# A Strassen-style scheme for four of six chunks of a decay attention with a two-layer softplus network

## The chip, the cores and the metric

The kernel runs on one core of a Trainium2 chip. The metric is the device time in microseconds (us) of one execution; the times given are medians over runs. The profile is of one execution, taken by the hardware profiler.

## What is computed

Causal attention with a per-head decay, for 4 batches, 8 heads, 768 positions and head size 64, block by block with a carried state, and then a two-layer network on all 3072 tokens:

```python
# per head: out = (q k^T * Dmask) v + (q * lam_pow) state ; state = lam^64 * state + (k * rev_pow)^T v
x = attn_out.transpose(0, 2, 1, 3).reshape(3072, 512)
h = x @ w_in                                            # 512 -> 2048
g = np.maximum(h, 0.0) + np.log1p(np.exp(-np.abs(h)))   # softplus
return g @ w_out                                        # 2048 -> 512
```

Everything is float32. The two layers do 2 x 3072 x 512 x 2048 multiply-adds.

## The kernel before, in words

The 768 positions are cut into six chunks of 128, so that a chunk has 512 tokens (4 batches x 128). In a chunk, attention is done in four units, one per pair of heads, numbered g = 4 x chunk + pair. Each unit has q, k and v in one SBUF tile of 8 KB per partition.

TensorE multiplies in float32r. To keep float32 accuracy, each operand is split in a high part (a copy rounded by ScalarE) and a low part (VectorE subtracts the high part from the original), and each block product is made from three matmuls: high x high, low x high, high x low. Weights are cut and split once, on the chip, in the first 115 us (`w_scale` to `w_lo`), and then stay in SBUF in sixteen tiles `w_pairs`, two blocks of 128 x 512 each.

The network runs in steps s = 0 to 95, sixteen per chunk. Step s does `mlp1(s)`, 12 matmuls of 512 columns that make 128 rows of the hidden layer in one PSUM bank, and, LAG = 4 steps later, `mlp2([s])`, 12 matmuls that add into four PSUM banks, one per batch. Between the two, `chain_act` (softplus), `chain_hi` (ScalarE) and `chain_lo` (VectorE) turn the bank into the next operand. `finish` does the last batch of the last two steps in two halves of 256 columns, so that each half can be stored on its own.

Up to step 16 the order of all instructions is a list written out by hand. From step 17 on, a loop sets it: at three places of each chunk it puts the next chunk's attention between the steps, `chunk_scores` at f = 3 and `chunk_outs` at f = 7. On each engine, and on SP's DMA queue, instructions run in the order in which the program emits them. Buffers come from pools: "b8" (22 tiles of 8 KB), "b4" (7 of 4 KB), and in PSUM "o" (4 banks), "h" (2 banks), "t" (one tile of 2 banks). GpSimd does ten small instructions at the start and nothing after.

## Time and profile before

| | |
|---|---|
| Time, median of 3 runs (lowest, highest) | 592.29 us (592.20, 592.38) |
| Profiled execution, first to last instruction (span) | 590.3 us |
| TensorE busy (4473 matmuls) | 585.0 us, 99% of the span |
| TensorE weight loads, which overlap the matmuls | 485.7 us, 82% |
| VectorE busy | 252.4 us, 43% |
| ScalarE busy | 233.5 us, 40% |
| GpSimd busy | 1.7 us |
| Moved by DMA | 48.89 MB, mean 83 GB/s |

The span is 1.99 us shorter than the median of the runs: what lies before the first and after the last instruction isn't in it. Matmuls are pipelined, so the mean length of one (390 ns) is longer than the distance from one to the next; the distance is read from the chain or from a window.

### The profile page before, as it was taken

Reading aid. Unit: us, or ns where it says so; the run is one execution under the profiler, and the core shown is the slowest. Engines: PE = TensorE matmul, PEld = TensorE weight load, DVE = VectorE, ACT = ScalarE, POOL = GpSimd, SP = SyncE. Lnnn points to the kernel's source line nnn. Section 1 sums busy time; section 2 is a strip of 40 time slices with the busy share of each in tenths; the row PEclk is TensorE's granted clock in tenths of the full one; section 3 lists DMA queues with packets and bytes.
Section 4 is the critical chain, followed back from the end, with each engine's and each line's share of the span. In section 5 each row is a group of like instructions: output and inputs, shape, how many; then the busy total and the mean of one; then the engine's idle time right before and its main releaser. Section 6 shows DMA issues by size and latency. Waiting matters only on the chain.

```text
span 590.3 us, 10279 instructions
## 1 busy us (share of the span) xinstructions
PE 585.0 (99%) x4473; PEld 485.7 (82%) x4473; DVE 252.4 (43%) x407; ACT 233.5 (40%) x391; POOL 1.7 (0%) x10
## 2 busy tenths in 40 slices
PE   8999999999999999999999999999999999999997
PEld 6878888888888888888888888888888888888886
DVE  7999999658411119621106841012842111201011
ACT  4999966562231363222246132225222122312212
POOL 1000000000000000000000000000000000000000
PEclk9999999999999999999999999999999999999999
DMA  8999502520300211030031030031100000100001
GB/s 298 407 406 410 192 1 73 214 74 1 144 0 1 92 52 73 2 143 1 0 144 72 1 144 1 1 116 44 57 1 2 0 1 0 72 0 1 0 1 71
DMA packets 13294, 48.89 MB, mean 83 GB/s; under 512 B 1474, under 2 KB 1730, under 8 KB 11074
## 3 DMA queue, kind: packets, MB, share of 16 engines
q1 hardware_dynamic: 12816, 47.58, 21.4%
q8 instruction: 35, 0.57, 0.4%
q10 hardware_dynamic: 434, 0.66, 0.3%
q14 instruction: 9, 0.07, 0.0%
HBM read 41.94 MB, written 6.29 MB: 82 GB/s over the span
## 4 chain that ended last, share of the span: by engine, by line
PE 93%; DMA 4%; ACT 2%; DVE 0%; issue 0%
PE o L522 44%; PE h L483 42%; PE z L353 3%; DMA att<-in_att 2%; PE x L322 2%; DMA raw<-in_wts 2%; PE w L322 1%; PE y L326 1%; ACT c L236 0%; ACT raw L240 0%; PE z L364 0%; ACT w L257 0%; PE e L495 0%; PE x L341 0%; PE z L368 0%; DVE w L261 0%
## 5 line engine op out<-in xcount | busy, mean ns | idle before, releaser
L483 PE MATMUL h<-x,w 128*128 128x512 f32 x1152 | 275.4, 390 | 0.2 <-DVE w L261 0.2
L522 PE MATMUL o<-w,g 128*128 128x512 f32 x1146 | 274.4, 390 | 0.0
L483 PEld LDWEIGHTS h<-x,w 128*128 128x128 f32 x1152 | 215.6, 188 | 45.7 <-DVE w L261 0.6
L522 PEld LDWEIGHTS o<-w,g 128*128 128x128 f32 x1146 | 214.6, 188 | 44.9
L472 DVE TENSOR_TENSOR g<-l,g 128x512 fp32r<-128x512 f32 x96 | 66.3, 691 | 308.2 <-ACT g L468 307.9
L464 ACT ACTIVATE l<-h 128x512 f32<-128x512 f32 x96 | 57.4, 598 | 297.2 <-PE h L483 272.2
L468 ACT CAST g<-l 128x512 fp32r<-128x512 f32 x96 | 59.5, 620 | 2.8
L299 ACT ACTIVATE att<-att,rp 64x256 f32<-64x256 f32 x60 | 27.0, 499 | 0.2
L310 DVE TENSOR_TENSOR att<-att,lp 64x512 f32<-64x512 f32 (+1 forms) x42 | 24.6, 585 | 1.1
L375 DVE TENSOR_TENSOR att<-x,mask 64x512 f32<-64x512 f32 (+1 forms) x34 | 19.1, 563 | 5.9 <-PE y L326 4.1
L257 ACT CAST w<-c 128x1024 fp32r<-128x1024 f32 (+1 forms) x19 | 17.2, 912 | 9.3 <-DVE c L254 9.2
L261 DVE TENSOR_TENSOR w<-c,w 128x1024 fp32r<-128x1024 f32 (+1 forms) x19 | 20.0, 1055 | 1.4 <-ACT w L257 1.3
L236 ACT ACTIVATE c<-raw 128x1024 f32<-128x1024 f32 (+1 forms) x19 | 18.9, 997 | 3.9 <-DMA raw<-in_wts 3.7
L254 DVE CUSTOM_DVE_ANT_0 c<-raw,c 128x2048 uint16<-128x2048 uint16 (+1 forms) x19 | 19.8, 1052 | 0.5 <-ACT raw L240 0.4
L248 DVE SCALAR_TENSOR_TENSOR c<-raw,c 128x1024 uint32<-128x1024 uint32 (+1 forms) x19 | 19.9, 1051 | 0.1
L240 ACT ACTIVATE raw<-raw 128x1024 uint32<-128x1024 uint32 (+1 forms) x19 | 18.8, 1005 | 0.0
L353 PE MATMUL z<-att 128*64 128x64 f32 x544 | 17.0, 223 | 0.0
L353 PEld LDWEIGHTS z<-att 128*64 128x64 f32 x544 | 16.3, 138 | 0.6 <-issue 0.4
L396 ACT COPY att<-st 64x512 f32<-64x512 f32 (+1 forms) x21 | 11.0, 535 | 12.2 <-PE y L326 11.3
L322 PEld LDWEIGHTS x<-att 64*64 64x64 f32 x416 | 12.9, 135 | 2.8 <-issue 2.8
L442 ACT CAST x<-z 128x512 fp32r<-128x512 f32 x17 | 9.2, 593 | 13.6 <-PE z L353 9.2
L322 PE MATMUL x<-att 64*64 64x64 f32 x416 | 14.1, 220 | 0.0
(77 smaller groups left out, 223.4 us busy)
## 6 DMA issues: line engine op xcount, KB each, us to landing
att<-in_att SPq DMA_DIRECT2D x17, 1024.0 KB, 6.4
raw<-in_wts SPq DMA_DIRECT2D x32, 512.0 KB, 10.1
out_dram<-ob SPq DMA_DIRECT2D x21, 256.0 KB, 2.5
att<-in_att SPq DMA_DIRECT2D x10, 512.0 KB, 9.6
att<-in_att SPq DMA_DIRECT2D x8, 256.0 KB, 8.7
out_dram<-ob ACTq DMA_DIRECT2D x2, 256.0 KB, 2.0
out_dram<-ob ACTq DMA_DIRECT2D x1, 128.0 KB, 1.8
out_dram<-ob SPq DMA_DIRECT2D x1, 128.0 KB, 1.7
```

The lines of the kernel that those rows point to most:

```text
L248: nc.vector.scalar_tensor_tensor(out=c, in0=raw_at(ks, 1), scalar=0x80000000, in1=c, op0=ALU.bitwise_and, op1=ALU.bitwise_or)
L254: nc.vector.tensor_add(out=c, in0=c, in1=raw_at(ks, 0))
L261: nc.vector.tensor_sub(out=w[:, 1], in0=conv.pop(ks[0]).bitcast(F32), in1=w[:, 0])
L299: nc.scalar.activation(k, k, AF.Copy, scale=rp1[r, h : h + 1])
L310: nc.vector.tensor_mul(out=q, in0=q, in1=w[r, bs])
L322: nc.tensor.matmul(x[to, cols], lhsT=region(g, s)[r, b, t], rhs=region(g, 1 - s)[r, b, t], start=True, stop=True)
L353: nc.tensor.matmul(w[half(t), cols], lhsT=region(g, 2 + s)[:, b, t], rhs=region(g, 1 - s)[:, b, t], start=True, stop=True,)
L464: nc.scalar.activation(l_tiles[s], h_tiles.pop(s), AF.Softplus)
L468: nc.scalar.copy(out=g_tiles[s][:, 0, :], in_=l_tiles[s])
L472: nc.vector.tensor_sub(out=g[:, 1, :], in0=l_tiles.pop(s), in1=g[:, 0, :])
L483: nc.tensor.matmul(h_tiles[s], lhsT=w[:, i, cs], rhs=x[:, j, :], start=p == 0 and n == 0, stop=p == NP - 1 and n == 2,)
L522: nc.tensor.matmul(o_tiles[c][b], lhsT=g[:, i, b * 128 : (b + 1) * 128], rhs=w[:, j], start=f == 0 and n == 0, stop=(f == NF - 1 or s == l ...
```

## The change

Chunks 0 and 1 and the first part of chunk 2's loads stay as they were, up to step 16 of the hand-written list. Chunks 2 and 3, and chunks 4 and 5, are each taken as a pair. In each layer of a pair, the matrices are cut in 2 x 2 blocks, and the product is made from seven block products in place of eight (Strassen's scheme in the form with shared sums).

- **Weights.** `keep` stores three of the seven weight operands of each layer to DRAM as they are. `prepare` makes the other four: GpSimd adds high and low parts of two blocks (2 x 512 columns) and makes four sums or differences (4 x 256 columns), ScalarE and VectorE split the result again, and SP stores it to DRAM. There are 16 such preparations, spread over steps 17 to 34 in program order. All seven operands are then streamed back from DRAM (`l1_load`, `l2_load`), in each pair anew.
- **First layer of a pair**, eight steps j: seven products of 6 matmuls each in three PSUM banks A, B, D. A bank takes a second product after ScalarE (`l1_copy`) or VectorE (`l1_sum`) has read the first. VectorE's sums make the four blocks, ScalarE's softplus runs on them (`soft`). The x operands are seven combinations made by `x_minus` and split by `x_block`.
- **Second layer of a pair**, seven products n in four parts of 12 matmuls: ScalarE and VectorE split the operand (`l2_split`), GpSimd makes the differences of blocks (`l2_minus`, 16 per pair, 1024 columns each), VectorE and ScalarE add up the results (`l2_end`), and SP stores them in four DMAs of 512 KB per pair (`l2_store`). Chunks 2 to 5 are written transposed and turned on the host when the results are collected.
- **Attention** of chunks 2 to 5 is done unit by unit: a burst on TensorE holds the outputs of the last unit and the scores of the next one, five bursts per chunk.
- **Order.** From step 17 on, operations are handed to a planner (`Plan`) with an engine, a booked duration, what they read and write, buffers and a due time. The planner plays them through when the program is built, each engine free to take what is ready, and emits them by the start times that it found. What it emits is fixed from then on.

The diff, cut to its core:

```diff
+    LATENCY = {"PE": 0.35, "ACT": 0.12, "DVE": 0.12, "POOL": 0.15, "SP": 0.1}
...
+                    soonest = min(found)[0]
+                    t, _, n = min((x for x in found if x[0] <= soonest + 0.05), key=lambda x: (x[1], x[2]))
+                    if best is None or t < best[0]:
+                        best = t, n
...
+            if e == "PE":
+                if o["kind"] != last_kind:
+                    dur += 0.14
+                last_kind = o["kind"]
+            free_at[e] = end = t + dur
+            if o["size"] is not None:
+                channel = max(channel, t) + o["size"] / 0.35
+                end = channel + 1.8
...
-    def chunk_scores(c):
...
-    def chunk_outs(c):
...
-    def finish(ss, cols, e, to):
...
+    w1d = dp.tile([NF // 2, 128, 7, 2, 256], F32, name="w1d")
+    w2d = dp.tile([7, 2, 128, 4, 2, 256], F32, name="w2d")
+    def keep(*ks):
+        for k in ks:
+            f, which = w_order[k]
+            w, (j, odd) = w_of(f, which).bitcast(F32), divmod(f, 2)
+            if which == 0:
+                to, of = (w1d[j][:, 2], w[:, :, 256:]) if odd else (w1d[j][:, 0:2].rearrange("q h n e -> q (h n) e").rearrange("q (n h) e -> q n (h e)", n=2), w)
+                nc.sync.dma_start(out=to, in_=of)
+            else:
+                for n, h in ((1, 0), (6, 1)) if odd else ((0, 0),):
+                    nc.sync.dma_start(out=w2d[n, j // 4][:, j % 4], in_=w[:, :, h * 256 : (h + 1) * 256])
...
+        10, shift 24 25, act 11, mlp 12, ghi 11, load 32, keep 1 0 2 3 5 6 7 4 8 9 10 11 12 13 14 15 16 17
+        18 19 20 21, xl1 5, out1 6, hi 22 23, glo 11, act 12, sign 24 25, round 30 31, lo 22 23, keep 22 23,
...
+        sign 28 29, ghi 14, shift 30 31, mlp 16, add 28 29, hi 28 29, unit 10, mlp 15, glo 14, lo 28 29,
+        keep 28 29, mlp2 11, sign 30 31, mlp2 12, mlp2 13, add 30 31, act 15, ghi 15, glo 15, hi 30 31, lo
+        30 31, keep 30 31
...
+    plan = Plan({"b8": 22, "b4": 7, "bl": 1, "bh": 5, "o": 4, "h": 2, "t": 1})
...
+    MM, R6, R12 = 0.2266, 6 * 0.2266, 12 * 0.2266
...
+    def act(n):
+        return 0.15 + 0.0009 * n
+    def dve(n):
+        return 0.16 + 0.00104 * n
+    def pool(n):
+        return 0.25 + 0.0022 * n
+    def ffn(dur, fn, reads, writes, alloc=()):
+        nonlocal clock
+        n = add("PE", dur, fn, reads, (*writes, ("ffn",)), alloc, due=clock)
+        clock += dur
+        return n
...
+    def prepare(which, j):
+        e, o = 2 * j, 2 * j + 1
...
+            nc.gpsimd.tensor_add(
+                out=T8[cs][:, 2 * n : 2 * n + 2].rearrange("q h e -> q (h e)"), in0=w[:, 0], in1=w[:, 1]
+            )
+        for n in range(2):
+            add(
+                "POOL", pool(512), lambda n=n: whole_of(n), [("wp", pairs[n][0])], [(*cs, 2 * n), (*cs, 2 * n + 1)],
+                [("b8", cs), ("b8", sk)] if n == 0 else (), due=due,
+                behind=prepared[-1] if n == 0 and prepared else None,
+            )
+        a11, a12, a21, a22 = (0, 1, 2, 3) if which == 0 else (0, 2, 1, 3)
+        for to, x, y, op in ((6, a21, a22, ALU.add), (7, 6, a11, ALU.subtract), (5, a11, a21, ALU.subtract), (4, a12, 7, ALU.subtract)):
+            def combine(to=to, x=x, y=y, op=op):
+                t = T8[cs]
+                nc.gpsimd.tensor_tensor(out=t[:, to], in0=t[:, x], in1=t[:, y], op=op)
+            add("POOL", pool(256), combine, [(*cs, x), (*cs, y)], [(*cs, to)], due=due)
+        four = [(*cs, n) for n in range(4, 8)]
+        def hi():
+            nc.scalar.copy(out=T8[sk][:, :, 0], in_=T8[cs][:, 4:8])
+        def lo():
+            nc.vector.tensor_sub(out=T8[sk][:, :, 1], in0=T8[cs][:, 4:8], in1=T8[sk][:, :, 0])
+        add("ACT", act(1024), hi, four, [(*sk, 0)], due=due + 6)
+        prepared.append(len(plan.ops))
+        add("DVE", dve(1024), lo, [*four, (*sk, 0)], [(*sk, 1)], due=due + 7)
+        if which == 0:
+            key, to = ("w1d", j), lambda: w1d[j][:, 3:7]
+        else:
+            key, to = ("w2d", j), lambda: w2d[2:6, j // 4, :, j % 4].rearrange("n q a e -> q n a e")
+        add(
+            "SP", 0.06, lambda: nc.sync.dma_start(out=to(), in_=T8[sk].bitcast(F32)), [(*sk, 0), (*sk, 1)], [key], size=1.05,
+            due=due + 8,
+        )
...
+        add("SP", 0.06, load, [], u_keys(g, "q", "k0", "k1", "kt2", "kt3", "v"), [("b8", ("U", g))], size=1.05, due=due, behind=bursts.get(g - 2))
...
+    def attention(c, dues):
+        first = c * NP
+        q = c // 2
+        for g in range(first, first + NP):
+            due = dues[g - first]
+            load_unit(g, due - 5)
+            keys_decay(g, due - 2.5)
+            parts = [scores(g)] if g == first else [outs(g - 1), scores(g)]
+            bursts[g] = burst(parts, due)
+            if g > first:
+                x_copy(g - 1, due + 2)
+            after_scores(g, due + 2)
+        burst([outs(first + NP - 1)], dues[NP])
+        x_copy(first + NP - 1, dues[NP] + 2)
+        end = dues[NP] + 3
+        if c % 2 == 0:
+            x_block(q, 0, c, 0, end)
+            x_block(q, 1, c, 2, end)
+        else:
+            b = c - 1
+            x_minus(q, (b, 0), (c, 0), (b, 0), end)
+            x_block(q, 4, b, 0, end)
+            x_block(q, 2, c, 2, end)
+            x_minus(q, (c, 0), (c, 2), (c, 0), end)
+            x_minus(q, (c, 2), (c, 2), (b, 0), end)
+            x_block(q, 5, c, 2, end)
+            x_block(q, 6, c, 0, end)
+            x_minus(q, (b, 2), (b, 2), (c, 2), end)
+            x_block(q, 3, b, 2, end)
...
+                W1[q, j, n] = t8([128, 4, 2, 256], F32R, f"wa{q}_{j}_{n}")
+                nc.sync.dma_start(out=W1[q, j, n].bitcast(F32)[:, : b - a], in_=w1d[j][:, a:b])
+            add(
+                "SP", 0.06, load, written(0, [j]), [("W1", q, j, n, 0)], [("b8", ("W1", q, j, n))], size=0.262 * (b - a),
+                due=clock - 7, behind=l1_ops.get((q, j - 2) if j > 1 else (q, -1)),
+            )
...
+    def l1_products(q, j, name, wn, xn, to, start):
+        n, i = divmod(wn, 4)
+        def run():
+            if start:
+                AB[q, j, to] = obank(f"{to}{q}_{j}")
+            w, x = W1[q, j, n][:, i], XB[q, xn]
+            if wn < 2:
+                w = W1[q, j, n][:, 0:2].rearrange("q h n e -> q (h n) e").rearrange("q (n h) e -> q n h e", n=2)[:, :, i]
+            for k in range(2):
+                for m, (a, b) in enumerate(((0, 0), (1, 0), (0, 1))):
+                    nc.tensor.matmul(
+                        AB[q, j, to], lhsT=w[:, a, k * 128 : (k + 1) * 128], rhs=x[:, b, k],
+                        start=start and k == 0 and m == 0, stop=k == 1 and m == 2, skip_group_check=not start,
+                    )
...
+    def l1_last(q, j):
+        l1_products(q, j, "P4", 2, 3, "B", False)
+        l1_sum(q, j, "u", "B", blk="21")
+        soft(q, "21", j)
+    l1_ops, l2_ops = {}, []
+    def l1(q, j):
+        l1_ops[q, j] = l1_products(q, j, "P1", 0, 0, "A", True)
+        l1_copy(q, j)
+        if j:
+            l1_last(q, j - 1)
+        l1_products(q, j, "P6", 6, 5, "B", True)
+        l1_sum(q, j, "u", "B", tmp="v")
+        l1_products(q, j, "P5", 5, 4, "D", True)
+        l1_sum(q, j, "u", "D", tmp="d")
+        l1_products(q, j, "P2", 1, 1, "A", False)
+        soft(q, "11", j, "A")
+        l1_products(q, j, "P7", 4, 6, "B", False)
+        l1_sum(q, j, "d", "B", blk="22")
+        soft(q, "22", j)
+        l1_products(q, j, "P3", 3, 2, "D", False)
+        l1_sum(q, j, "v", "D", blk="12")
+        soft(q, "12", j)
+        if j == NF // 2 - 1:
+            l1_last(q, j)
...
+            W2[q, n, h] = t8([128, 4, 2, 256], F32R, f"wb{q}_{n}_{h}")
+            nc.sync.dma_start(out=W2[q, n, h].bitcast(F32), in_=w2d[n, h])
+        add(
+            "SP", 0.06, load, [k for k in written(1, range(4 * h, 4 * h + 4))], [("W2", q, n, h, 0)],
+            [("b8", ("W2", q, n, h))], size=1.05, due=clock - 7, behind=l2_ops[-5] if len(l2_ops) > 4 else l1_ops[q, 6],
+        )
...
+    def l2_minus(q, jp, to, x, y, due):
+        def minus():
+            nc.gpsimd.tensor_sub(out=l_pair(q, to, jp), in0=l_pair(q, x, jp), in1=l_pair(q, y, jp))
+        add("POOL", pool(1024), minus, lks(q, x, jp) + lks(q, y, jp), lks(q, to, jp), due=due)
...
+            G2[key] = t8([128, 2, 2, 512], F32R, f"gb{q}_{n}_{jp}")
+            nc.scalar.copy(out=G2[key][:, 0], in_=l_pair(q, blk, jp))
+        def low():
+            nc.vector.tensor_sub(out=G2[key][:, 1], in0=l_pair(q, blk, jp), in1=G2[key][:, 0])
+        add("ACT", act(1024), high, lks(q, blk, jp), [(*key, 0)], [("b8", key)], due=clock - 4, behind=l2_ops[-4] if len(l2_ops) > 3 else l1_ops[q, 6])
+        add("DVE", dve(1024), low, [*lks(q, blk, jp), (*key, 0)], [(*key, 1)], due=clock - 2)
...
+            for k in range(2):
+                for m in range(2):
+                    for r, (a, b) in enumerate(((0, 0), (1, 0), (0, 1))):
+                        nc.tensor.matmul(
+                            E2[q, n][m], lhsT=w[:, 2 * (jp % 2) + k, a, m * 128 : (m + 1) * 128], rhs=G2[key][:, b, k],
+                            start=jp == 0 and k == 0 and r == 0, stop=jp == 3 and k == 1 and r == 2,
+                        )
...
+    def l2_store(q, name, c, dh):
+        def run():
+            nc.sync.dma_start(
+                out=out[c, dh * 256 : (dh + 1) * 256].rearrange("(m q) i -> q m i", m=2), in_=OB[name][1]
+            )
...
+        c = 2 * q
+        for jp in range(4):
+            if n == 2:
+                pass
+            if jp % 2 == 0:
+                l2_load(q, n, jp // 2)
+            l2_split(q, n, jp)
+            l2_ops.append(l2_products(q, n, jp))
+            if n == 1:
+                l2_minus(q, jp, "11", "12", "11", clock)
+                l2_minus(q, jp, "12", "22", "12", clock)
+            if n == 2:
+                l2_minus(q, jp, "22", "22", "11", clock + 10)
+                l2_minus(q, jp, "21", "22", "21", clock + 20)
...
+    for s in range(17, 36):
+        if s < 32:
+            chain(s - 1) if s > 17 else chain(16)
+        if s == 32:
+            chain(31)
+        if 18 <= s:
+            if s < 34:
+                classic2([s - 4])
+            elif s == 35:
+                classic2([30, 31], [[b] for b in range(B)])
+            if s - 4 == 15:
+                classic_out(0)
+        if s < 32:
+            classic1(s)
+        if s == 18:
+            attention(2, [clock + 10.9 * n for n in range(5)])
+        if s == 26:
+            attention(3, [clock + 7.5 * n for n in range(5)])
+        if s % 2 == 1 and s < 33:
+            prepare(0, (s - 17) // 2)
+        if s % 2 == 0 and 20 <= s:
+            prepare(1, (s - 20) // 2)
+    classic_out(1)
+    for q in range(1, NCH // 2):
+        l1_ops[q, -1] = l2_ops[-4] if l2_ops else None
+        l2_ops.clear()
+        for j in range(NF // 2):
+            l1_load(q, j)
+            l1(q, j)
+            if q < NCH // 2 - 1 and j == 0:
+                attention(2 * q + 2, [clock + 14 * n for n in range(5)])
+        for n in range(7):
+            l2(q, n)
+            if q < NCH // 2 - 1 and n == 0:
+                attention(2 * q + 3, [clock + 10 * n for n in range(5)])
+    plan.run()
```

## Rows read from the trace of the kernel before

**Rows 1.** The page, part 1: busy time, share of the span, instructions.

```profile
PE 585.0 (99%) x4473; PEld 485.7 (82%) x4473; DVE 252.4 (43%) x407; ACT 233.5 (40%) x391; POOL 1.7 (0%) x10
```

**Rows 2.** Busy time in stretches: start:end, length, each engine, granted clock, DMA, GB/s.

```profile
115.40:590.30 474.90, 471.61 (x3411) 393.06 (x3409) 145.56 (x259) 144.33 (x258) 0.00 (x0) 1.00 0.11 41
317.20:412.60 95.40, 95.40 (x771) 79.62 (x771) 34.05 (x62) 28.63 (x52) 0.00 (x0) 1.00 0.15 56
...
108.00:112.00 4.00, 4.00 (x19) 3.34 (x18) 3.45 (x5) 1.64 (x3) 0.00 (x0) 1.00 0.96 352
```

**Rows 3.** The chain that ended last: by engine (page), pieces (start, us, what).

```profile
PE 93%; DMA 4%; ACT 2%; DVE 0%; issue 0%
...
115.41 2.72 PE h L483 x12
...
221.74 0.20 PE x L322
221.95 0.04 PE x L322
...
225.16 5.67 PE h L483 x24
230.83 5.44 PE o L522 x24
...
247.77 3.88 PE z L353 x128
251.66 2.97 PE o L522 x12
...
585.58 1.44 PE e L495 x12
```

**Rows 4.** Groups by line and shape: total us, mean ns, idle before.

```profile
L472 DVE TENSOR_TENSOR g<-l,g 128x512 fp32r<-128x512 f32 x96 | 66.3, 691 | 308.2 <-ACT g L468 307.9
L464 ACT ACTIVATE l<-h 128x512 f32<-128x512 f32 x96 | 57.4, 598 | 297.2 <-PE h L483 272.2 <-DVE g L472 23.9 <-DVE c L248 0.9
...
L310 DVE TENSOR_TENSOR att<-att,lp 64x512 f32<-64x512 f32 x26 | 17.9, 687 | 0.7
...
L261 DVE TENSOR_TENSOR w<-c,w 128x1024 fp32r<-128x1024 f32 x13 | 15.9, 1225 | 1.4 <-ACT w L257 1.3
...
L257 ACT CAST w<-c 128x1024 fp32r<-128x1024 f32 x13 | 13.7, 1050 | 9.3 <-DVE c L254 9.2
```

**Rows 5.** The order of time: SP's queue, the end, and GpSimd at the start.

```profile
67.97 0.92 SPq L133 DMA_DIRECT2D raw<-in_wts  x2
...
587.05 0.42 DVE L499 TENSOR_TENSOR ob<-e,ob 128x256 f32<-128x256 f32 x1 [0.22 <-PE e L495]
587.54 0.33 SPq L501 DMA_DIRECT2D out_dram<-ob  x1
...
1.14 0.10 POOL L178 MEMSET spare<- 128x8 f32 x1
...
1.21 0.51 POOL L180 MEMSET begin<- 128x512 f32 x1
1.78 0.54 POOL L181 MEMSET begin<- 128x8 f32 x1
```

**Rows 6.** DMA issues of the page: count, KB each, median us to landing.

```profile
att<-in_att SPq DMA_DIRECT2D x17, 1024.0 KB, 6.4
...
out_dram<-ob SPq DMA_DIRECT2D x21, 256.0 KB, 2.5
...
out_dram<-ob SPq DMA_DIRECT2D x1, 128.0 KB, 1.7
```

More of the change, by code (lines that the diff above doesn't have):

```diff
@@ new lines, in wk, with classic2, chain @@
+    def wk(f, which):
+        return [("wp", w_order.index((f, which)) // 2)]
+    def classic2(ss, parts=(range(B),)):
+        c, f = divmod(ss[0], NF)
+        for bs in parts:
+            ffn(
+                len(ss) * len(bs) * 3 * MM, lambda bs=bs: mlp2(ss, bs),
+                [k for s in ss for k in ((("g", s)), *wk(s % NF, 1))], [("o", c, b) for b in bs],
+                [("o", ("o", c, b)) for b in range(B)] if f == 0 else (),
+            )
+    def chain(s):
+        due = clock + 3
+        add("ACT", 0.6, lambda: chain_act(s), [("h", s)], [("l", s)], [("bl", ("l", s))], due=due)
+        add("ACT", 0.62, lambda: chain_hi(s), [("l", s)], [("g", s, 0)], [("b4", ("g", s))], due=due)
+        add("DVE", 0.69, lambda: chain_lo(s), [("l", s), ("g", s, 0)], [("g", s, 1), ("g", s)], due=due)
@@ new lines, in l2_end, with run @@
+    def l2_end(q, name, n, of=None, op=ALU.add, due=1.0):
+        for m in range(2):
+            def run(m=m):
+                if name not in OB or OB[name][0] != q:
+                    OB[name] = q, t4([128, 2, 512], F32, f"{name}{q}")
+                to = OB[name][1][:, m]
+                if of is None:
+                    nc.scalar.copy(out=to, in_=E2[q, n][m])
+                else:
+                    nc.vector.tensor_tensor(out=to, in0=OB[of][1][:, m], in1=E2[q, n][m], op=op)
+            key = ("OB", q, name)
+            add(
+                "ACT" if of is None else "DVE", 0.69, run,
+                [("E2", q, n, m, 0), *([] if of is None else [("OB", q, of, m)])], [(*key, m)],
+                [("b4", key)] if m == 0 and of != name else (), due=clock + due,
+            )
@@ L743 @@
         )
[L744 removed]
+    o = nc.dram_tensor("out_dram", (NCH, 512, 512), F32, kind="ExternalOutput").ap()
     with tile.TileContext(nc) as tc:
```

502 lines of the change are left out of this document (389 added, 113 removed).

## The prediction

> **What bounds the kernel now.** I read the page first: TensorE is busy 585.0 of 590.3 us, VectorE and ScalarE some 40%, GpSimd not at all [rows 1]. Busy time of matmuls may hide gaps, so the chain of waits comes next: 93% of what ended last is TensorE [rows 3]. Then the windows: from step 17 (115.4 us) to the end, TensorE is busy 471.61 of 474.90 us; the missing 3.29 us are the tail after the last matmul [rows 2]. So from there on only TensorE's work and the tail count, and the clock is granted at the upper of its two levels, 2.4 GHz (1.00). The pieces of the chain give the price: 12 matmuls of 512 columns last 2.72 us, 0.2267 us each, in both layers [rows 3]. A steady chunk lasts 95.40 us [rows 2]; 32 pieces of 2.72 are 87.04, so attention takes 8.36 us of TensorE per chunk.
>
> The other engines have room: in that chunk VectorE is busy 34.05 and ScalarE 28.63 of 95.40 us, and the DMA engines stand at 0.15 [rows 2].
>
> **What is removed and added on TensorE.** Four chunks took 4 x 384 matmuls. A pair now takes 8 x 7 x 6 in the first layer and 7 x 4 x 12 in the second, 672, and two pairs 1344. That is 192 fewer: **-43.5 us**. The split of the last step into halves goes too (1.44 for 1.36 us, -0.1) [rows 3].
>
> Attention keeps its matmuls but comes in five bursts per chunk, not two: 12 more interruptions. One costs 0.23 to 0.25 us in the piece behind it (5.67 for 5.44, 2.97 for 2.72) and perhaps 0.15 at entry (a first step of 0.20 against the usual 0.04 to 0.06) [rows 3]. Between 0.25 and 0.4, I take 0.3, as the entry step may be matmul time: **+3.6 us** (3.0 to 4.8).
>
> **The tail.** Before, the last matmuls end near 587.0 us, and 0.42 us of VectorE and a store of 128 KB (1.7 us to landing) follow [rows 3, 5, 6]. After, VectorE adds 512 columns (0.69, [rows 4]) and `l2_store` sends 512 KB. A 128 KB store lands in 1.7 and a 256 KB one in 2.5 us [rows 6], so 512 KB costs between 2.5 and 4.1 (0.8 for each doubling or for each 128 KB); I take 3.4. **+2.0 us** (1.1 to 2.7).
>
> Sum without any stall: 590.3 - 43.5 - 0.1 + 3.6 + 2.0 = 552.3 us of span, and with the 1.99 us by which the runs' median exceeds the profiled span **554.3 us**.
>
> **What has to stay hidden, and what it costs if it doesn't.** Prices: 0.69 us for VectorE on 512 columns, 1.23 on 1024; 0.60 and 1.05 for ScalarE [rows 4].
>
> *First layer of a pair.* A step j lasts 42 x 0.2267 = 9.5 us on TensorE; ScalarE has a copy and four softplus (3.0 us), VectorE five sums (3.45). Bulk fits; the distances are short. Bank B takes P7 two products (2.72 us) after P6, and `l1_sum` must have read it between: 0.25 to wake plus 0.69. One other VectorE instruction of 1.23 us ahead still fits (2.2), two don't, and each such case costs some 0.7 us. The planner orders sums by due time, so I expect few.
>
> *Second layer.* Per product of 2.72 us ScalarE has 1.05 and VectorE 1.23, and the split may run four products ahead. Hidden.
>
> *DMA.* `l1_load` moves 1.84 MB per 9.5 us, `l2_load` 1.05 MB per 5.4 us, both 194 GB/s; 352 GB/s flowed at a share of 0.96 [rows 2], and 1 MB lands in 6.4 us [rows 6], less than the 13.6 to 19 us by which loads may run ahead. `keep`'s 12.6 MB are 36 us at 352 GB/s, and fall between 68 us, when SP issues its last weight load [rows 5], and 115. Hidden, unless buffers are short (below). Each issue takes SP 0.33 us [rows 5] where the planner books 0.06: some 110 issues in 430 us, no bound.
>
> *Changes of phase* (classic to first layer, and three between layers): each has one result to fetch from a bank before a product, behind at most one 0.69 us operation, with other products between. 0 to 1.5 us each; I take 0.6, **+2.5**.
>
> *GpSimd.* Here is the unknown. A preparation is two operations on 512 columns and four on 256, booked at 2 x 1.38 + 4 x 0.81 = 6.0 us, and the next one waits (`behind`) until ScalarE (1.05) and VectorE (1.23) have split this one; with 0.5 for hand-overs that is 8.8 us, 140 us for 16. TensorE reaches the first layer of the first pair about 115.4 + 33 x 2.72 + 2 x 9.3 (8.36 and three more bursts) = 224 us and the second at 309, so the data itself is some 40 us early. What is not early is the queue: ScalarE's and VectorE's halves of a preparation stand between `chain_act` and `chain_lo` of the steps at a place fixed by the booked price. If GpSimd is late, ScalarE waits in line, the bank of h isn't emptied, and with two h banks TensorE stops some 7 us later.
>
> The only GpSimd rows write one operand and read none: 0.51 us for 512 columns, and 0.54 for eight [rows 5]. At the first price a preparation takes some 2 us; with 0.54 fixed and three times 1.0 ns per column (two reads, one write) it is 2 x 2.08 + 4 x 1.31 = 9.4 us, 3.4 over the booking. I take the booked 6.0, which lies between these ends, and for small lateness **+2.5** (0 to 10).
>
> The Trainium skill has a price: "GPSIMD Engine Reference", section 3.1, gives 4497 ns for adding two float32 tensors of 2048 elements per partition, an estimate of 1.1 us for 512 and 0.55 for 256 if taken in proportion, 4.4 us a preparation. By it GpSimd would be ahead of the plan and the 2.5 us fall away: 556.8. No run here shows it.
>
> The likeliest case: 554.3 + 2.5 + 2.5 = **559 us**, its own range 553 to 566.
>
> **Rivals.**
>
> *A: GpSimd and VectorE get in each other's way.* If a VectorE instruction with both inputs in SBUF and a GpSimd instruction can't run together, then in the 108 us of the classic part VectorE's 18 `chain_lo` (12.4), 16 half decays of q (11), 7 splits and 5 differences of x (14.8) compete with GpSimd, 38 us, 3.1 per 8.8 us. Half fits while GpSimd waits for its split; 1.6 us don't, ten times: 16, less the 7 us of slack, 9. In the second layer 16 `l2_minus` of 2.5 us meet a split of 1.23 per product: 1.0 us over TensorE's 2.72 each time, 16 less the lead of 10.9, 5 per pair. Together 19: 554.3 + 2.5 + 19 = **576**. No row speaks for it, since GpSimd rests wherever VectorE is loaded. The Trainium skill says so outright ("SBUF — State Buffer", section "Who interferes with whom"): a VectorE instruction with two SBUF inputs and a GpSimd instruction that reads SBUF share a port that is locked for a whole instruction. No run here shows it, as GpSimd does nothing after 3 us. By that rule A would be the likeliest case; as the traces so far bear it out, its chance is 0.19.
>
> *B: too few 8 KB buffers when the first pair starts.* At 224 us some 12 of 16 preparations are done. Four weight tiles, two for the running preparation, seven x operands, four hidden blocks and three of attention are 20 of 22; a step's `l1_load` wants two, and two steps ahead want four. If loads run only one step ahead, each waits for a buffer and then 6.4 us for landing; some 5 us a step for the four steps until preparations end: +20, **577**. Against it: dues of loads precede most others. Chance 0.11.
>
> *C, the other side: slower than before.* GpSimd at the upper price. Every preparation then makes ScalarE wait 3.4 us beyond the booked place: 16 x 3.4 - 7 = 47 us, **604**. The point from which it decides: the sum must lose 592.3 - 556.8 = 35.5, so (35.5 + 7)/16 = 2.7 us per preparation, 8.7 us of GpSimd in place of 6.0. Against it: the upper price counts 0.54 us of fixed cost per instruction, but another memset of eight columns took 0.10 us [rows 5]. Chance 0.12.
>
> That the work isn't saved at all is excluded: the matmuls are counted in the code.
>
> **Numbers.** Forecast 0.58, A 0.19, B 0.11, C 0.12. The range runs from 551 (3.0 and 1.1 for the bursts and the tail, no stalls, and 1 us for what I can't see) to 580, which holds A and B with all but their worst; left out are C and some 0.06 of the rest. 0.2%, 1.2 us, is about what a measurement of this kernel can tell from no change. Slower: 0.10 of C; same: 0.02 of C; faster: the rest, 0.88.
>
> **What would show it.** 192 fewer matmuls of 512 columns, still at 0.227 us from start to start; five bursts per chunk; a last store of 512 KB behind 0.69 us of VectorE. In the forecast TensorE's busy share stays at 99% from 115 us on, and its waits sum to under 12 us. A shows as GpSimd operations well above 1.4 and 2.5 us, or VectorE's two-input operations above 0.69 and 1.23, wherever the two overlap. B shows as first-layer matmuls near 224 to 260 us waiting for a DMA, and SP waiting for a buffer. C shows as ScalarE's split of prepared weights waiting for GpSimd, with softplus queued behind. The prediction is wrong if TensorE has gaps that none of these explains, for instance gaps that the planner's own layout leaves.

## The result, and the profile after

The changed kernel takes 568.85 us (median of 4 runs, 567.39 to 568.95), the kernel before 592.25 beside it: a ratio of 0.9602, 95% interval 0.9588 to 0.9615. The forecast of 559.0 us was 9.9 too low; the range of 551 to 580 holds the time. The profiled execution took 567.39 us with a span of 565.6, against 557.3 of span in the working of the forecast (552.3 and the two allowances of 2.5). So 8.3 us are to be found there, and 1.5 more lie between this execution and the median.

Part 1 of the page of the changed kernel and its chain by engine; they answer to [rows 1, 3]:

```profile
PE 549.1 (97%) x4275; PEld 449.6 (79%) x4275; DVE 426.5 (75%) x498; ACT 288.7 (51%) x420; POOL 215.8 (38%) x138
...
PE 36%; DVE 10%; issue 2%; DMA 1%; ACT 0%; ACTq 0%; DVEq 0%
```

There are 198 matmuls fewer: the 192, and six more that went with the split into halves. VectorE rose from 43% to 75%. The chain of what ended last can be followed back only to 279.3 us here, so its shares add up to half of the span; VectorE's is 10%, where it was 0. The same stretch as in [rows 2], from step 17 to the end (here step 17 begins at 114.73 us):

```profile
115.40:565.60 450.20, 436.83 (x3210) 357.67 (x3208) 316.72 (x350) 200.89 (x291) 205.68 (x124) 1.00 0.58 217
```

450.20 less 436.83 is 13.4 us without a matmul, 4.4 of them the tail. The other 9.0 are what the list of TensorE's waits shows (us in total, times, the longest):

```profile
PE e L1217 <- DVE gb L1202: 2.8, 2, 2.3
PE B L1075 <- DVE xb L996: 2.6, 2, 2.1
PE h L608 <- ACT xs L981: 1.3, 1, 1.3
PE B L1075 <- ACT xb L993: 1.1, 1, 1.1
PE z L509 <- DVE att L971: 1.0, 1, 1.0
PE B L1075 <- DVE uv L1122: 0.2, 1, 0.2
```

The reader sees that no DMA is among them, nor GpSimd. TensorE waits for VectorE: for its split of a second-layer operand (L1202), of an x operand (L996), for the decay of q (L971). What makes VectorE late stands in its groups, total us and mean ns:

```profile
L1202 DVE TENSOR_TENSOR gb<-l,gb 128x1024 fp32r<-128x1024 f32 x56 | 97.3, 1774 | 6.7 <-ACT gb L1199 6.6
L971 DVE TENSOR_TENSOR att<-att,lp 64x512 f32<-64x512 f32 x32 | 31.6, 989 | 0.5
L597 DVE TENSOR_TENSOR g<-l,g 128x512 fp32r<-128x512 f32 x32 | 28.8, 899 | 17.6 <-ACT g L593 17.3
L946 DVE TENSOR_TENSOR att<-w,mask 64x512 f32<-64x512 f32 x32 | 22.0, 688 | 0.6
L996 DVE TENSOR_TENSOR xb<-xs,xb 128x1024 fp32r<-128x1024 f32 x14 | 20.6, 1470 | 1.7 <-ACT xb L993 1.6
...
L1122 DVE TENSOR_TENSOR l<-B,d 128x512 f32<-128x512 f32 x16 | 11.0, 690 | 19.9 <-PE B L1075 19.8
```

The split of 1024 columns has a mean of 1774 ns against 1225 in [rows 4], the split of g 899 against 691, the decay 989 against 687. All of these read two operands from SBUF. `l1_sum` (L1122) and the mask (L946) have one operand in PSUM and one in SBUF, and stay at 690 and 688. GpSimd's side, tile by tile (minimum, median, maximum in ns):

```profile
L1190 POOL TENSOR_TENSOR l<-l,l x32: 2397/3350/6359, 310.9 to 522.0; 128x1024 f32<-128x1024 f32 x32
```
```profile
L880 POOL TENSOR_TENSOR cs<-cs x64: 723/741/2586, 111.4 to 294.3; 128x256 f32<-128x256 f32 x64
L866 POOL TENSOR_TENSOR cs<-w x32: 1262/1297/2295, 106.9 to 290.2; 128x512 f32<-128x512 f32 x32
```

Left alone, GpSimd takes 2.40, 1.27 and 0.73 us, a little under the booked 2.50, 1.38 and 0.81; the largest values are two to three times that. The order of time shows both at once, VectorE first, then GpSimd (start, us):

```profile
321.36 9.73 DVE L1202 TENSOR_TENSOR gb<-l,gb 128x1024 fp32r<-128x1024 f32 x3 [0.28 <-ACT gb L1199]
331.12 2.78 DVE L971 TENSOR_TENSOR att<-att,lp 64x512 f32<-64x512 f32 x1
```
```profile
319.95 16.22 POOL L1190 TENSOR_TENSOR l<-l,l 128x1024 f32<-128x1024 f32 x5
```

Three splits take 9.73 us, 3.24 each, and five differences 16.22, also 3.24 each; the ones at the edges are disturbed for only a part of their time. In between they alternate: the differences begin at 319.95, 323.29, 326.63 and 329.96 us, the splits at 324.33 and 327.68, 3.34 or 3.35 us apart. Alone they need 1.22 and 2.40, 3.62 together, so a pair overlaps by some 0.3 us and is otherwise one after the other. That is rival A's mechanism. The Trainium skill, "SBUF — State Buffer", section "Who interferes with whom", states it: a VectorE instruction with two SBUF inputs and a GpSimd instruction that reads SBUF contend for a shared port; a VectorE instruction with at most one SBUF input, outside its two-port modes, doesn't. The rows here agree on both halves, though a pair overlaps by the 0.3 us.

The tail, from the order of time (VectorE, then SP's queue); it answers to the end in [rows 5]:

```profile
560.60 1.37 DVE L1237 TENSOR_TENSOR U<-U,e 128x512 f32<-128x512 f32 x2 [5.99 <-PE e L1217]
```
```profile
562.00 0.37 SPq L1247 DMA_DIRECT2D out_dram<-U  x1
```

The first sum runs as soon as the first result bank is ready, the second when the last matmul has ended, at 561.24 us. From there to the end it is 4.4 us: 0.8 to the issue of the store, 2.8 to its landing and 0.8 after that. Before it was 3.3.

### The profile page after: what moved, and what is told of

The parts are those of the page before. It is cut to its first block, busy times and chain, and to the rows that moved or that the text cites. A ratio compares the mean times of both kernels' runs of the same rounds, so it can differ in the third digit from the quotient of the medians.

```text
span 565.6 us, 10346 instructions
## 1 busy us (share of the span) xinstructions
PE 549.1 (97%) x4275; PEld 449.6 (79%) x4275; DVE 426.5 (75%) x498; ACT 288.7 (51%) x420; POOL 215.8 (38%) x138
## 5 line engine op out<-in xcount | busy, mean ns | idle before, releaser
L1217 PE MATMUL e<-gb,wb 128*128 128x512 f32 x672 | 156.4, 393 | 2.8 <-DVE gb L1202 2.8
L1190 POOL TENSOR_TENSOR l<-l,l 128x1024 f32<-128x1024 f32 x32 | 104.2, 3281 | 126.2 <-DVE gb L1202 125.6
L1217 PEld LDWEIGHTS e<-gb,wb 128*128 128x128 f32 x672 | 126.7, 189 | 30.3 <-DVE gb L1202 3.6
L1202 DVE TENSOR_TENSOR gb<-l,gb 128x1024 fp32r<-128x1024 f32 x56 | 97.3, 1774 | 6.7 <-ACT gb L1199 6.6
L608 PE MATMUL h<-x,w 128*128 128x512 f32 x384 | 92.2, 392 | 1.3 <-ACT xs L981 1.3
L622 PE MATMUL o<-w,g 128*128 128x512 f32 x384 | 92.4, 392 | 0.0
L608 PEld LDWEIGHTS h<-x,w 128*128 128x128 f32 x384 | 71.5, 188 | 16.8 <-ACT xs L981 1.5
L622 PEld LDWEIGHTS o<-w,g 128*128 128x128 f32 x384 | 71.5, 188 | 15.2
L1075 PE MATMUL B<-xb,wa 128*128 128x512 f32 x288 | 71.9, 392 | 3.9 <-DVE xb L996 2.6
L880 POOL TENSOR_TENSOR cs<-cs 128x256 f32<-128x256 f32 x64 | 61.8, 980 | 2.5
L971 DVE TENSOR_TENSOR att<-att,lp 64x512 f32<-64x512 f32 x32 | 31.6, 989 | 0.5
```

The costliest lines, as they stand in the source:

```text
L608: nc.tensor.matmul(h_tiles[s], lhsT=w[:, i, cs], rhs=x[:, j, :], start=p == 0 and n == 0, stop=p == NP - 1 and n == 2,)
L622: nc.tensor.matmul(o_tiles[c][b], lhsT=g[:, i, b * 128 : (b + 1) * 128], rhs=w[:, j], start=f == 0 and n == 0, stop=f == NF - 1 and n == 2,)
L880: nc.gpsimd.tensor_tensor(out=t[:, to], in0=t[:, x], in1=t[:, y], op=op)
L971: nc.vector.tensor_mul(out=q, in0=q, in1=w[r])
L1075: nc.tensor.matmul(AB[q, j, to], lhsT=w[:, a, k * 128 : (k + 1) * 128], rhs=x[:, b, k], start=start and k == 0 and m == 0, stop=k == 1 and ...
L1190: nc.gpsimd.tensor_sub(out=l_pair(q, to, jp), in0=l_pair(q, x, jp), in1=l_pair(q, y, jp))
```

## Where the time went

From the starts of the stages on TensorE a balance can be drawn. Ideal is 2.72 us for 12 matmuls and the 9.26 us that the prediction allowed for the attention of a chunk with its bursts: 108.3 us for the classic part (step 17 to the first layer of the first pair), 85.4 for each layer of the first pair, 152.3 for the second pair. The profiled execution has 110.7, 91.1, 92.3 and (to the last matmul) 152.5. So 2.4, 5.6 and 6.8 us are lost, and in the second pair, where GpSimd and VectorE do the same second-layer work but no attention is left, next to nothing.

The table has the lengths of the stages in the profiled execution of each run, in us; "end" is the second pair to the end of the span. Each median is that of the timed runs, each ratio is to the kernel before on the same chip, with its 95% interval. The runs e0 to e3, e4 to e7, and e8 and e9 are from three chips, on which the kernel before took 592.00, 591.81 and 591.84 us.

| run | classic | layer 1 | layer 2 | end | median | ratio |
|---|---|---|---|---|---|---|
| changed kernel, first profile | 110.7 | 91.1 | 92.3 | 156.9 | 568.85 | 0.9602 (0.9588 to 0.9615) |
| e0, the same again | 110.7 | 93.9 | 90.7 | 156.9 | 569.13 | 0.9614 (0.9598 to 0.9629) |
| e1, GpSimd only writes | 110.7 | 88.2 | 87.1 | 156.9 | 559.96 | 0.9463 (0.9449 to 0.9478) |
| e2, differences only write | 110.7 | 93.7 | 87.1 | 156.9 | 565.39 | 0.9547 (0.9526 to 0.9569) |
| e3, attention of chunk 5 thinner | 110.7 | 93.8 | 88.0 | 156.9 | 565.25 | 0.9545 (0.9523 to 0.9566) |
| e4, other due times | 109.5 | 92.5 | 92.8 | 156.9 | 570.29 | 0.9640 (0.9626 to 0.9655) |
| e5, e4 and a shorter tail | 109.5 | 94.0 | 93.2 | 156.1 | 569.30 | 0.9621 (0.9606 to 0.9635) |
| e6, e4 and GpSimd only writes | 109.5 | 87.6 | 86.0 | 156.9 | 556.89 | 0.9416 (0.9402 to 0.9430) |
| e7, matmuls in the wait | 110.7 | 91.0 | 90.7 | 156.9 | 567.50 | 0.9593 (0.9577 to 0.9609) |
| e8, e3 and e7 | 110.7 | 91.1 | 88.0 | 156.9 | 563.26 | 0.9519 (0.9506 to 0.9532) |
| e9, e8 and a shorter tail | 110.7 | 91.4 | 88.0 | 156.1 | 562.75 | 0.9505 (0.9492 to 0.9518) |

## The experiments

**e0: the changed kernel again**, as the reference for those that follow.

> The changed kernel once more, on the chip of the next three runs, as the point that they are compared with. Both theories: 567 to 570 us, TensorE some 14 us short of its own work between step 17 and the last matmul, and waits in the same places (200, 220 to 250, 320 to 394 us).

569.13 us (567.88 to 569.74). The first layer of the first pair is 2.9 us longer here than in the first profile, and the second 1.6 shorter. The windows around the wait at 228 us (start:end, length, PE, PEld, DVE, ACT, POOL, granted clock, DMA share, GB/s) show why. The first profile:

```profile
228.00:232.00 4.00, 0.79 (x6) 0.30 (x3) 4.00 (x5) 3.60 (x5) 0.59 (x1) 1.00 0.02 8
232.00:236.00 4.00, 4.00 (x17) 3.30 (x18) 3.97 (x7) 1.05 (x1) 3.98 (x3) 1.00 0.55 227
236.00:240.00 4.00, 4.00 (x19) 3.33 (x18) 3.91 (x7) 1.10 (x2) 2.82 (x4) 1.00 0.27 102
```

e0:

```profile
228.00:232.00 4.00, 0.77 (x5) 0.33 (x3) 4.00 (x4) 3.60 (x5) 0.57 (x1) 0.90 0.02 5
232.00:236.00 4.00, 4.00 (x10) 3.17 (x11) 3.03 (x5) 1.05 (x1) 4.00 (x3) 0.50 0.56 229
236.00:240.00 4.00, 4.00 (x15) 3.24 (x14) 2.88 (x4) 0.00 (x0) 2.62 (x4) 0.75 0.26 100
```

After the same wait, in which TensorE does only 0.8 us of work in 4, the granted clock falls in e0 to 0.50, the lower of its two levels (1.2 GHz), and TensorE starts 25 matmuls in 8 us instead of 36. Eleven at 0.2267 are 2.5 us. So the wait costs itself and, in some executions, 2.5 to 2.9 us more. In the first profile it happens elsewhere, behind a wait of 2.3 us that ends at 393.9 us; 22% and 21% of two windows are some 1.7 us, and e0, with the same wait there and a clock of 1.00, is 1.6 shorter in that layer:

```profile
392.00:396.00 4.00, 2.13 (x6) 1.70 (x7) 4.00 (x5) 0.54 (x1) 0.00 (x0) 0.78 0.00 0
396.00:400.00 4.00, 4.00 (x16) 3.19 (x15) 3.77 (x7) 0.00 (x0) 0.00 (x0) 0.79 0.08 30
```

The granted clock over a whole execution was 0.996 in the first profile and in one more of eight executions of this kernel, and 0.993 or 0.994 in the other six.

**e1: GpSimd only writes.** The port tested: each GpSimd operation that reads SBUF is replaced by two fills of the same tile, so that the order, the waits and the buffers stay. Weights and differences are left out by it.

```diff
...
-                nc.gpsimd.tensor_tensor(out=t[:, to], in0=t[:, x], in1=t[:, y], op=op)
+                for _ in range(2):
+                    nc.gpsimd.memset(t[:, to], 0.25)
...
-            nc.gpsimd.tensor_sub(out=l_pair(q, to, jp), in0=l_pair(q, x, jp), in1=l_pair(q, y, jp))
+            for _ in range(2):
+                nc.gpsimd.memset(l_pair(q, to, jp), 0.25)
```

> Every two-input operation of GpSimd from step 17 on is replaced by two memsets of the same destination, so that GpSimd writes at the same places of its queue and reads nothing; weights and differences are thus left out, all other engines keep their work and their order. Theory P (the 14 us that TensorE loses are due to GpSimd and VectorE blocking each other when both read SBUF): VectorE's splits go back to 1.22 us from a mean of 1.77, its q decays to 0.69 from 0.99, and 9 to 14 us are won: 555 to 560. Theory L (most of the 14 us is in the order and due times laid out by the planner, the blocking adds only what VectorE is late beyond that): the durations go back just the same, but only 2 to 5 us are won: 564 to 567.

559.96 us, 9.2 below e0 and in theory P's range. The groups of VectorE and the fills of GpSimd in e1:

```profile
L1203 DVE TENSOR_TENSOR gb<-l,gb 128x1024 fp32r<-128x1024 f32 x56 | 66.2, 1218 | 17.1 <-ACT gb L1200 17.1
...
L971 DVE TENSOR_TENSOR att<-att,lp 64x512 f32<-64x512 f32 x32 | 21.9, 685 | 4.5 <-PE w L478 4.1
```
```profile
L1191 POOL MEMSET l<- 128x1024 f32 x64 | 59.6, 956 | 161.2 <-DVE gb L1203 159.4
```

Every VectorE operation is back at its own price; the 56 splits alone give back 31 us. GpSimd also works less than before, since a pair of fills takes 1.91 us where a difference takes 2.40, so some of the gain could be GpSimd being early; no run here separates the two. But no GpSimd operation stood in TensorE's waits before, and the waits that shrink are VectorE's: those for gb go from 2.8 to 0.7 us, those for xb from 3.7 to 1.1. And the chain of the changed kernel that leads to the wait at 393.9 us is VectorE's from 324 us on, but for two operations of ScalarE, without GpSimd. The classic part stays at 110.7 us to a tenth, although 16 of its splits of g had taken a mean of 1078 ns: there the stretching was hidden.

**e2: only the differences in the second layer write** (the second half of e1's edit).

> Only the 32 differences of the second layers are replaced by memsets (the differences are left out); the 16 preparations keep their reads. Theory P: what was lost at 316 to 409 us, 6.8 us, comes back, 560 to 562, and the loss of the first pair's first layer (5.7 us at 225 to 317) stays. Theory L: 2 to 3 us come back in that stretch, 565 to 567, and TensorE still waits near 378 and 392.

565.39 us, 3.7 below e0. That is theory L's range, not theory P's: of the 6.8 us, 3.6 come back, since the rest was bursts, the clock's fall and a wait of 0.7 us that stays near 392. But the second layer of the first pair is as short as in e1, 87.1 us, and the first layer as long as in e0. So the port's cost has two places: the differences beside attention in the second layer (3.6 us), and the last preparations beside the x operands at the start of the first (5.5 us in the profiles, 93.7 for 88.2, of which the clock's fall at 232 us is the 2.5 to 2.9 of e0). That place, in the changed kernel's order of time on VectorE (three of its operations), then GpSimd's preparation:

```profile
221.81 2.13 DVE L1004 TENSOR_TENSOR xs<-xs 128x1024 f32<-128x1024 f32 x1 [1.35 <-ACT xs L981]
...
224.59 1.74 DVE L996 TENSOR_TENSOR xb<-xs,xb 128x1024 fp32r<-128x1024 f32 x1
...
227.93 1.75 DVE L996 TENSOR_TENSOR xb<-xs,xb 128x1024 fp32r<-128x1024 f32 x1
```
```profile
220.08 2.77 POOL L866 TENSOR_TENSOR cs<-w 128x512 f32<-128x512 f32 x2 [1.96 <-PE z L509]
222.94 5.66 POOL L880 TENSOR_TENSOR cs<-cs 128x256 f32<-128x256 f32 x4
```

The chain of differences and splits of x (1.21 us each when alone) has no slack there: TensorE has begun the first layer and waits at 228 us for its operands. Counted from the first product, the split that it waits for ends 2.3 us later than in e1, and 0.8 of that was there when the chain began. There the lateness came another way: ScalarE copies the x block (L981) behind an operation that waits for a load until 220.1 us, and SP had issued that load at 211.5, behind the store of a preparation whose split VectorE ended at 211.1. Seen from the first product both are 0.7 later than in e1.

**e3: the attention of chunk 5 spread out.** If the port costs only where VectorE is full, thinning VectorE's other work should help with the port untouched.

```diff
-                attention(2 * q + 3, [clock + 10 * n for n in range(5)])
+                attention(2 * q + 3, [clock + 14 * n for n in range(5)])
```

> One number is changed: the due times of the attention of chunk 5, which runs beside the first pair's second layer, are 14 us apart, not 10. GpSimd's and VectorE's work is the same. Theory P: the same operations share the same port in the same stretch, so at most 1 us is won: 567 to 569. Theory L: VectorE's bunch of attention before the splits thins out, 3 to 5 us of the 6.8 lost at 316 to 409 come back: 563 to 566.

565.25 us, 3.9 below e0, as much as e2: theory L's range, and theory P's limit of 1 us is refuted. The second layer takes 88.0 us for 90.7, and TensorE's waits in it fall from 3.8 us in e0 (2.8 for gb, 1.0 for the decay of q) to

```profile
PE e L1217 <- DVE gb L1202: 1.4, 2, 0.8
```

The stretching hasn't gone: the splits take a mean of 1915 ns, more than the 1774 of e0. So in the second layer the loss comes from attention, splits and stretching together on a VectorE that is full, and one of them can be moved.

**e4: a layout with other due times throughout**, meant to remove the waits of the phases.

```diff
-            [("b8", ("W2", q, n, h))], size=1.05, due=clock - 7, behind=l2_ops[-5] if len(l2_ops) > 4 else l1_ops[q, 6],
+            [("b8", ("W2", q, n, h))], size=1.05, due=clock - 7, behind=l2_ops[-6] if len(l2_ops) > 5 else l1_ops[q, 6],
...
-                l2_minus(q, jp, "22", "22", "11", clock + 10)
+                l2_minus(q, jp, "22", "22", "11", clock + 0)
...
-            attention(2, [clock + 10.9 * n for n in range(5)])
+            attention(2, [clock + 9 * n for n in range(5)])
...
-            attention(3, [clock + 7.5 * n for n in range(5)])
+            attention(3, [clock - 3 + 7.5 * n for n in range(5)])
...
-                attention(2 * q + 2, [clock + 14 * n for n in range(5)])
+                attention(2 * q + 2, [clock + 8 + 11 * n for n in range(5)])
...
-                attention(2 * q + 3, [clock + 10 * n for n in range(5)])
+                attention(2 * q + 3, [clock + 5 + 13 * n for n in range(5)])
```

> Only due times and one limit on prefetch are changed: attention of chunk 2 every 9 us for 10.9, of chunk 3 begun 3 us earlier, of chunk 4 every 11 us from 8 us later, of chunk 5 every 13 us from 5 us later, second-layer weights up to six products ahead, one difference due earlier. GpSimd's and VectorE's work is the same. Theory P, the port alone: 1 us at most, 567 to 569. Theory L with P (port and order each hold a part): some 6 us less than the changed kernel, 561 to 564; the wait near 228 us stays.

570.29 us: this failed, e4 is no faster than e0. Both theories' ranges miss it. It gains 1.2 us in the classic part and 1.5 in the first layer, and loses 2.1 in the second. The 1.5 is the clock's: the wait at 228 us lasts 3.1 us, where e0 has 3.2, but the clock falls to 0.73 in the window behind it, not to 0.50. In the second layer the waits are gathered in a single one, of 4.9 us, and the clock falls behind it. TensorE's waits in e4, and the windows:

```profile
PE e L1217 <- DVE gb L1202: 4.9, 1, 4.9
```
```profile
364.00:368.00 4.00, 1.15 (x4) 0.91 (x5) 4.00 (x3) 0.00 (x0) 1.72 (x1) 0.91 0.14 18
368.00:372.00 4.00, 4.00 (x40) 2.93 (x39) 2.83 (x4) 1.99 (x2) 0.00 (x0) 0.66 0.87 352
```

**e5: e4 with a shorter tail.** In the last step the products of one result bank end before those of the other, and the last 512 KB are stored in two halves.

```diff
-            for k in range(2):
-                for m in range(2):
+            final = q == NCH // 2 - 1 and n == 6 and jp == 3
+            for m, k in ((0, 0), (0, 1), (1, 0), (1, 1)) if final else ((0, 0), (1, 0), (0, 1), (1, 1)):
...
-            l2_store(q, "U", c, 1)
+            if q < NCH // 2 - 1:
+                l2_store(q, "U", c, 1)
+                return
+            for m in range(2):
+                rows = slice(256 + m * 128, 384 + m * 128)
+                add(
+                    "SP", 0.06, lambda m=m, rows=rows: nc.sync.dma_start(out=out[c, rows], in_=OB["U"][1][:, m]),
+                    [("OB", q, "U", m)], [], size=0.262, due=clock + 3,
+                )
```

> As the run before, and the end is cut in two: the last twelve matmuls finish one bank after the other, and the last 512 KB are stored in two DMAs of 256 KB, each when its half is there. If the tail is worth what its rows say (0.7 us of VectorE and the difference between a 512 KB and a 256 KB store), 0.8 to 1.6 us less than the run before. If the landing of a store doesn't depend on its size, 0.5 us or less.

569.30 us, 1.0 below e4, with intervals that overlap. In the profiles the stretch from the second pair's start to the end is 0.7 us shorter (156.13 for 156.85). The 5.0 us of tail in e9's expectation below is a wrong reading: it counts from the end of the first result bank; from the last matmul it is 4.4, and 3.6 with this edit.

**e6: e4 with GpSimd only writing** (e1's edit on e4).

> The changed due times, and GpSimd's two-input operations replaced by memsets as in the first write-only run (weights and differences are left out). If port and order are separate parts of the loss: 3 to 5 us less than that run, 555 to 557. If both act through one queue, VectorE's, so that either remedy frees it: within 1.5 us of that run's 560.

556.89 us, 13.4 below e4 and 3.1 below e1, whose interval lies clear of it. That is the range for two separate parts, but they don't add, since e4 alone gained nothing. So e4's due times are better than the kernel's own, but only where GpSimd and VectorE don't hold each other up; with the port in place the gain turns into the one long wait. The planner books 2.50 and 1.23 us for operations that together take 3.34 a pair, so its times don't hold beside the port.

**e7: matmuls in the wait.** Is it the low activity in the wait at 228 us that costs the clock? Twelve matmuls are put there, into a bank that the next product overwrites.

```diff
+            if (q, j, name) == (1, 0, "P6"):
+                for _ in range(12):
+                    nc.tensor.matmul(AB[q, j, to], lhsT=w[:, 0, 0:128], rhs=XB[q, 0][:, 0, 0], start=True, stop=True)
```

> The changed kernel with twelve more matmuls in front of the first pair's second product, in the 3.2 us in which TensorE otherwise waits for the split of x near 228 us; they write the bank that the product then overwrites. Theory C (the wait there lets TensorE's clock fall to 1.2 GHz for the next 8 us or so, as the granted clock of 0.50 at 232 to 236 us shows, and that costs 2.8 us in most runs): 565.5 to 567, granted clock 1.00 in that stretch. Against it (the fall of the clock costs nothing, since VectorE is late there anyway): 568 to 570.

567.50 us, 1.6 below e0 with intervals that overlap, and between the ranges of the two theories; in the profile the first layer takes 91.0 us for 93.9. The windows of e7:

```profile
228.00:232.00 4.00, 3.46 (x19) 2.54 (x15) 4.00 (x4) 2.80 (x5) 1.65 (x2) 1.00 0.02 6
232.00:236.00 4.00, 4.00 (x17) 3.29 (x18) 3.97 (x7) 1.51 (x2) 3.98 (x3) 1.00 0.55 227
```

VectorE is as full as before and the operands come no earlier, yet the clock stays at 1.00. One profile isn't enough to show that the matmuls did it, as the first profile had 1.00 here without them (and a first layer of 91.1 us). The clock over whole executions says more: it was 0.999, 0.999, 0.996 and 0.997 in e7's four, for the 0.993 to 0.996 of the unchanged kernel's eight. The 2.9 us of this profile are more than the 1.6 of the medians, since the clock doesn't fall here in every execution of the unchanged kernel and can fall elsewhere in e7.

**e8: e3 and e7 together; e9: e8 with e5's tail.**

> The dues of attention(5) 14 apart instead of 10 (e3) and twelve extra matmuls into bank B in the wait near 228 us (e7, their products are overwritten) together. If the two gains are of separate kinds they add: the later attention gave 3.9 us in the second layer of the first pair, the filling 1.6 us in the first, so 569.1 - 5.5 = 563.6 us (562 to 565), the first layer of the first pair at 90.5 to 91.5 us and the granted clock at 1.00 near 232 us. The rival: the planner's order in the second layer hangs on what came before, or the clock falls at another wait instead; then it stays at 565 to 567, as each of the two alone.

> As e8, and in the last step the products for one bank of the result end before those of the other, and the last 512 KB are stored as two times 256 KB, each behind its own sum. In e5 the time from the last matmul to the end fell from 5.0 to 3.6 us by this. If the tail is what it looks like it gives 1.0 to 1.4 us here too: 1.2 below e8, about 562.4 us. If the end is set by the last transfer whatever its size, there is no difference to e8.

e8 takes 563.26 us (563.16 to 563.58), 0.3 from the sum of the two gains, so they seem to be of separate kinds. The ratios of e8 and e3 have intervals that overlap, but each of e8's four times lies below each of e3's (563.96 to 566.36). The clock is 1.00 throughout 224 to 244 us, and over whole executions 0.998 to 1.000 in the nine of e8 and e9, for 0.992 to 0.997 in e3's four: with the matmuls in the wait the clock stays up. TensorE's waits after 115 us shrink from 9.1 us in e0 to 3.9, but 2.7 of that is the time of the twelve matmuls themselves. e9 takes 562.75 us; its interval overlaps e8's, so the tail's 0.7 us in the profile isn't shown as a gain of its own, and the 1.2 expected was too much. e9 is the fastest version that computes all: 6.4 us below e0, 5.0% below the kernel before.

## Why the prediction was right or wrong, point by point

**Matmuls (-43.5) and their price: right.** The second pair, free of attention, takes 152.5 us for 672 matmuls, 0.227 each.

**Bursts (+3.6): too small by 2.5.** I took 9.26 us for the attention of a chunk. The middle bursts in the classic part (timeline of TensorE):

```profile
126.93 2.88 PE L608 MATMUL h<-x,w 128*128 128x512 f32 x12
129.74 1.15 PE L509 MATMUL z<-att 128*64 128x64 f32 x32
131.91 3.04 PE L622 MATMUL o<-w,g 128*128 128x512 f32 x12
134.79 2.88 PE L608 MATMUL h<-x,w 128*128 128x512 f32 x12
```

The piece from 126.93 ends its 2.72 us at 129.65; the next one starts at 131.91 and is 0.16 longer than usual (3.04 for 2.88): 2.42 us. Three of these, with the first burst (1.32 by the same count) and the last (1.31), are 9.89 a chunk, 2.5 more for four. The step that failed is the price of 0.3 for each of the 12 added interruptions; with the measured 6.1 us in all it is 0.51.

**Tail (+2.0): +1.1 measured**, the lower end. The store of 512 KB landed in 2.8 us, not the 3.4 that I took; the time from landing to the end, about 1 us, is in both tails.

**Phase changes (+2.5): near in sum, by luck.** In e1, where no port is shared, TensorE's waits are 3.1 us, but only 1.1 of them stand at a change of phase (229 and 238 us), and for a split of x, not for a result in a bank. The other 2.0 are a step that waits for ScalarE's copy of x at 202 us (1.3) and a split in the second layer at 387 us (0.7): gaps of the planner's own layout, which the prediction gave as a sign of being wrong.

**GpSimd's lateness (+2.5): this step failed.** GpSimd's own price, undisturbed, was a little under the booked one, and GpSimd is never what TensorE waits for. A preparation alone takes 2 x 1.27 + 4 x 0.73 = 5.5 us. What the term left out is the price that VectorE pays: 9.2 us of the median by e1, with the clock and with whatever GpSimd being early adds. I had weighed this as rival A, with 0.19, because no row before could show it. That e1, without it, comes so near the forecast of 559 is in part luck: bursts that I took 2.5 too low stand against a tail 0.9 and waits 1.9 lower than allowed (3.1 for 5.0). The Trainium skill's rule ("SBUF — State Buffer", "Who interferes with whom") would have been the better guide, and e1 shows what it states: with GpSimd only writing, nothing is blocked.

**Rival A: mechanism as described, place and size not.** I put 9 us in the classic part and 5 in the second layer of each pair. It is nothing in the classic part, nothing in the second pair, 3.6 us in the first pair's second layer, and the rest in its first. What I missed is that the stretching costs only where VectorE is behind for longer than the splits' lead lasts, or where, as at the start of the first layer, there is no lead. The first pair's second layer up to 392 us, and the fullest stretch of the second pair's:

```profile
316.51:392.00 75.49, 73.58 (x599) 59.73 (x597) 73.60 (x65) 38.83 (x50) 51.19 (x15) 1.00 0.59 217
508.00:530.00 22.00, 22.00 (x98) 18.22 (x98) 22.00 (x13) 8.42 (x9) 17.40 (x6) 1.00 0.83 312
```

With attention VectorE is busy (its blocked time counted in) 73.6 of 75.5 us. In the second pair it is full too, 22.0 of 22.0 us, but TensorE doesn't miss a matmul: the splits may run four products, 10.9 us, ahead. The prediction's own sum gives this with the measured price: a pair is 3.34 - 2.72 = 0.6 us over TensorE's pace, not 1.0, so 16 are 10 us, within the lead (an estimate). In the first pair attention's work on VectorE comes on top.

**Rivals B and C: refuted.** No wait for a DMA stands in TensorE's list after 115 us; ScalarE's split waited five times for a preparation, 5.4 us in all against the 54 (16 x 3.4) of rival C, and TensorE's list shows nothing of it; with VectorE in its way a preparation took 7.0 us on average (2 x 1.53 + 4 x 0.98), over the booked 6.0 but under the 8.7 from which C decides.

**The clock: not in the prediction at all.** I had every gap cost its own length. In the profiled execution the fall at 394 us cost 1.7; in others the one at 232 costs 2.5 to 2.9, the likely source of the 1.5 between profile and median.

The balance of the profiled execution is bursts +2.5, waits 9.0 for the 5.0 allowed, so +4.0, clock +1.7, tail -0.9: 7.3 of 8.3. Two more terms are in the rows. Step 17 began at 114.73 us, 0.5 earlier than before (115.25). And a wait costs more than its idle time: a matmul lasts 0.39 us where the next follows after 0.227, and the idle time counts from its end, so each of the eight waits loses an estimated 0.16 more, 1.3 in all. With these it is 8.1 of 8.3. Open is how much of e1's gain is the port itself and how much that fills are shorter than differences; and whether a GpSimd operation with one input blocks in the same way wasn't tried.

## What to carry to other kernels

Before GpSimd is given idle work, look at what VectorE does at the same time: if its instructions read two operands from SBUF, book the pair at nearly the sum of both (3.34 us for 1.22 and 2.40 here), and put GpSimd's work where VectorE has slack for longer than the lead of what it feeds. A gap on TensorE can cost nearly as much again through the clock (gaps of 2.3 to 4.9 us cost up to 2.9 more here, and in some executions nothing), so spread waits or fill them. And where a planner lays out the order, its prices should come from a profile in which both engines work before its due times are tuned: e4's better layout was worth 3.1 us without the shared port and nothing with it. A plan with corrected prices wasn't tried.

## What the runs showed of the hardware

- VectorE's two-input operation of 1024 columns (1.22 us alone) and GpSimd's (2.40) took 3.34 us a pair when both were always ready. Fills on GpSimd (0.96 us for 1024 columns, 0.31 for 256) left VectorE's 1.22 unchanged.
- VectorE's operations with one operand in PSUM stayed at 0.67 to 0.70 us beside a busy GpSimd.
- GpSimd's price without disturbance: 0.73, 1.27 and 2.40 us for two inputs of 256, 512 and 1024 float32 columns.
- The same wait of TensorE led to a granted clock of 0.50 in one execution and to no fall in another. With 12 matmuls in the wait, and attention spread out, the clock over whole executions was 0.998 to 1.000 in nine of nine, and without the matmuls 0.992 to 0.997 in four of four.
- An idle time shown between two matmuls understates what the wait costs, by an estimated 0.16 us here: a matmul of 512 columns lasts 0.39 us and the next one follows after 0.227.
